# Expert pairs: where one block difference is issued on VectorE, ahead of an addition or behind it

## The chip, the cores and the metric

The kernel runs on one core of one Trainium2 chip. The metric is the device time of one execution in microseconds (us); a time is the median of several executions. The engines are TensorE (PE in the rows; PEld is its weight load), VectorE (DVE), ScalarE (ACT), GpSimd (POOL) and the queue of DMA issues (SP).

## The reference, cut to what matters

Three stages follow each other: an attention over pooled keys, a mixture of eight experts whose gate is balanced by eight rounds of row and column scaling, and a feed-forward layer with softplus. The change lies in the second, whose core is

```python
    out = np.zeros((N, D), dtype=np.float32)
    for e in range(E):
        h = np.maximum(x @ w1[e], 0.0)
        ye = h @ w2[e]
        out += P[:, e:e + 1] * ye
```

with N = 2304 tokens, D = 512, E = 8 experts and 1024 hidden features each.

## The kernel before

The tokens are cut into three groups of 768. Each group passes the experts once, and the hidden features are taken in units of 256, so that one group has 32 units. Every matrix product is made of three matmuls, of a rounded part ("hi") and a remainder ("lo") of either operand. The first product of a unit, x @ w1, is done by a seven-product scheme for 2 x 2 blocks (Strassen and Winograd): with four blocks of the weights and four of the tokens, seven block products named A11, A22, S2, S1, A12, S3 and S4 take the place of eight. Each is six matmuls of 384 columns, and the additions of their results are done on VectorE.

For the second and third group the kernel goes by pairs of units (`first_twice`, `second_twice`): the second product, h @ w2, is done by the same scheme over the two units of a pair. The pair's four blocks of h and three sums of them are then the seven operands ("forms") of seven form products of twelve matmuls each. There are 16 pairs in a group, 32 in all, and they lie between 640 and 1556 us of the span, apart from the very first units.

The order of issue is written out by hand. For a pair d the sequence is: first product of its even unit, form products 2 to 6 of the pair before, first product of its odd unit, form products 0 and 1 of pair d, first product of the even unit of pair d + 1, and so on. Each engine takes its instructions in this order and waits in front of one whose data are not there.

`first_twice` has two double-bank tiles d1 and d2 of PSUM from a pool of two buffers per kind; pairs take the kinds "R" and "L" in turn, and a form product takes its tile py from a pool of the same two kinds. The products are issued as A11, A22, S2, S1, A12, S3; S4 is issued later, behind the next form product (`go_on`). S2 and then S3 accumulate in the same bank pb. The addition u (`vadd(u1, pb, a)`, line 868) must read S2's result there before S3 is added to it. In the code it stands behind the product S1. In the rows it is `u<-p,za` at line 845.

When the odd unit's blocks are finished, `odd_posts` makes the forms. It puts four steps into a list `later`, which the first product of the next even unit works off:

- s2 copies s3 (a difference of two blocks, made shortly before) to its hi part on ScalarE and takes the remainder on GpSimd;
- s4 subtracts s3 from d1 on VectorE, in PSUM (`p<-p,s`, line 846), and copies the result to the hi part of form 6 on ScalarE;
- s1 adds d2 to a21 on VectorE (`a<-p,a`, line 845), takes the hi part on ScalarE and the remainder on GpSimd. It is the last reader of d2;
- the fourth takes the remainder of form 6 on VectorE (`hlo<-p,hhi`, line 896). It is the last reader of d1.

In the odd units `later` is empty. The last pair's four steps are worked off by a unit of the third stage, in `first`, which issues s4 behind its own addition u.

Of the kernel before, what the change touches and what calls it, by code (L numbers as in the profile page):

```python
# [19 lines left out]
def attention_moe_softplus_kernel(  # L20
# [800 lines left out]
    def product_of(n):  # L821

        whi, wlo = w1_t.pop(n)

        def product(ps, a, b, onto=False):
            hi, lo = xs[b]
            for c in range(2):
                three(
                    ps, (whi[:, a, c, :], wlo[:, a, c, :]), (hi[:, c, :], lo[:, c, :]),
                    c == 0 and not onto, c == 1, onto,  # L830
                )

        return product

    two_t = {}
    later = []

    def run_later():
        while later:
            later.pop(0)()  # L840

    def two_banks(kind, name):
        return banks[kind].tile([P, 2, 512], F32, tag=f"two{kind}", name=name)[:, :, :TB]
# [4 lines left out]
    def first_twice(n, between):  # L848

        product = product_of(n)  # L850
        a, u1 = (zpool.tile([P, TB], F32, tag="z", name=x) for x in ("za", "u1"))
        kind = "RL"[sets[n][3] // 2 % 2]
        d1 = two_banks(kind, "p")
        pa, pd_ = d1[:, 0], d1[:, 1]
        product(pa, A11, "b11")
        between(0)
        product(pd_, A22, "t4")
        nc.scalar.copy(a, pa)
        between(1)
        for _ in range(2):  # L860
            if later:
                later.pop(0)()
        d2 = two_banks(kind, "p")
        pc, pb = d2[:, 0], d2[:, 1]
        product(pb, S2, "t2")
        between(2)
        product(pc, S1, "t1")
        vadd(u1, pb, a)
        run_later()
        between(3)  # L870
        product(pa, A12, "b21", True)
        between(4)
        product(pb, S3, "t3", True)
        vadd(a, pb, a)
        vadd(pb, pc, a)
        vadd(pd_, pd_, a)
        between(5)
        two_t[n] = d1, d2

        def s4():  # L880
            product(pc, S4, "b22", True)
            vadd(pc, pc, u1)

        return s4
# [678 lines left out]
    for step, (what, n) in enumerate(todo):  # L1563
# [3 lines left out]
        if what == "first":  # L1567
# [10 lines left out]
            if twice(n):  # L1578
# [10 lines left out]
                def between(k):  # L1589

                    for _ in range((0, 1, 0, 1, 1, 3)[k]):
                        if to_split:
                            to_split.pop(0)()
                    if u % 2 == 0:
                        if k == 2:
                            settled()
                        if joins and k == 1:
                            joins.pop(0)()
                        return
                    if joins and k == 2:  # L1600
                        joins.pop(0)()
                    if k == 0:
                        sharing[0] = not side
                        pause[0] = 0
                    if not sharing[0]:
                        hook()
                    elif (k == 0 and (u < NU1 - 1 or twice(n + 1))) or not between_chunks[0]:
                        convert()

                away[0] = "LR"[u // 2 % 2]  # L1610
                rest = first_twice(n, between)
                prep_w1(n + 1)
                load_w(1, n + 2)
# [124 lines left out]
```

## Time and profile before

| | us |
|---|---|
| median of 3 runs | 1955.16 |
| lowest and highest run | 1954.87, 1958.92 |
| the profiled execution | 1954.04 |
| its span | 1952.3 |
| TensorE busy in the span | 1928.6 (99%) |
| VectorE busy | 1471.4 (75%) |
| GpSimd busy | 1475.1 (76%) |
| ScalarE busy | 973.6 (50%) |

The busy shares are averages over stages with different limits. Matmuls overlap, and their ends are modelled: each is recorded with about 0.33 us, while they start 0.173 us apart when nothing holds them. The granted clock is 0.999 over the span.

### The profile page before, as it was taken

The numbers are of one execution on the slowest core, as the hardware profiler recorded it, in microseconds if no ns is written. First come the engines' busy times: TensorE is split into PE (matmuls) and PEld (weight loads), VectorE is DVE, ScalarE is ACT, GpSimd is POOL, SyncE is SP. The second block draws the span as 40 slices with busy tenths as digits, with TensorE's granted clock in tenths as the row PEclk, the third lists the DMA queues.
The fourth block names the chain that finished last, engine by engine and source line by source line (L and its number), as shares of the span: only waits on it lengthen the run. The fifth ranks groups of instructions, "written<-read, shape, count | busy, mean of one in ns | idle before, by whom it ended". The sixth has DMA issues, their size and how long they took to land.

```text
span 1952.3 us, 30469 instructions
## 1 busy us (share of the span) xinstructions
PE 1928.6 (99%) x10954; PEld 1794.4 (92%) x10954; DVE 1471.4 (75%) x2339; ACT 973.6 (50%) x1773; POOL 1475.1 (76%) x1142
## 2 busy tenths in 40 slices
PE   9899999999999999999999999999999999999999
PEld 7687888989989999999999999999999999999997
DVE  7775576887667888878988889888789776556455
ACT  6545435433334545545445655455554565565542
POOL 6776667787877788778787798887787879675563
PEclk9999999999999999999999999999999999999999
DMA  7343434555547655554555655555545523523311
GB/s 205 116 150 125 145 125 136 178 178 173 183 151 260 208 165 166 168 181 150 163 176 160 219 168 167 161 174 165 181 153 163 192 93 122 191 89 119 133 65 65
DMA packets 213347, 306.56 MB, mean 157 GB/s; under 512 B 33308, under 2 KB 147532, under 8 KB 212940
## 3 DMA queue, kind: packets, MB, share of 16 engines
q1 hardware_dynamic: 203116, 290.85, 46.4%
q10 hardware_dynamic: 10080, 13.77, 1.9%
q8 instruction: 86, 1.41, 0.3%
q14 instruction: 65, 0.53, 0.1%
HBM read 239.30 MB, written 65.27 MB: 156 GB/s over the span
## 4 chain that ended last, share of the span: by engine, by line
PE 90%; DVE 3%; POOL 2%; ACT 2%; DMA 1%; issue 1%; SPq 0%; ACTq 0%; DVEq 0%; POOLq 0%
PE py L797 45%; PE p L797 42%; POOL w1lo L289 1%; PE px L522 1%; PE s L477 1%; DMA vt<-in_v_dram 1%; PE pa L512 1%; DMA pb<-pd 0%; DVE p L1045 0%; POOL w2lo L289 0%; ACT w1hi L320 0%; DMA w2raw<-td 0%; PE pq L464 0%; ACT xhi L693 0%; DVE za L1045 0%
## 5 line engine op out<-in xcount | busy, mean ns | idle before, releaser
L797 PE MATMUL p<-xhi,w1hi 128*128 128x384 f32 x1680 | 572.7, 341 | 5.1 <-DVE p L1045 1.3
L797 PE MATMUL p<-xlo,w1hi 128*128 128x384 f32 x1680 | 563.0, 335 | 0.1
L797 PE MATMUL p<-xhi,w1lo 128*128 128x384 f32 x1680 | 562.9, 335 | 0.0
L289 POOL TENSOR_TENSOR w2lo<-w2raw,w2hi 128x512 fp32r<-128x512 f32 (+1 forms) x235 | 364.0, 1566 | 113.0 <-ACT w2hi L243 100.0
L289 POOL TENSOR_TENSOR w1lo<-w1raw,w1hi 128x512 fp32r<-128x512 f32 x240 | 239.6, 1021 | 227.0 <-ACT w1hi L320 226.9
L797 PEld LDWEIGHTS p<-xhi,w1hi 128*128 128x128 f32 x1680 | 315.6, 188 | 30.1 <-DVE u L845 14.0
L797 PEld LDWEIGHTS p<-xlo,w1hi 128*128 128x128 f32 x1680 | 315.7, 188 | 5.0 <-DVE xlo L1399 0.4
L797 PEld LDWEIGHTS p<-xhi,w1lo 128*128 128x128 f32 x1680 | 315.5, 188 | 0.0
L289 POOL TENSOR_TENSOR w1lo<-sums,w1hi 128x1024 fp32r<-128x1024 f32 x120 | 289.1, 2409 | 1.9 <-ACT w1hi L320 1.9
L797 PE MATMUL py<-w2hi,hhi 128*128 128x512 f32 x672 | 266.4, 396 | 3.3 <-DVE kbd L420 1.3
L797 PE MATMUL py<-w2hi,hlo 128*128 128x512 f32 x672 | 264.0, 393 | 0.0
L797 PE MATMUL py<-w2lo,hhi 128*128 128x512 f32 x672 | 263.6, 392 | 0.0
L797 PE MATMUL py<-hhi,w2hi 128*128 128x384 f32 x716 | 239.4, 334 | 1.1 <-ACT whi L243 1.1
L797 PE MATMUL py<-hlo,w2hi 128*128 128x384 f32 x716 | 239.2, 334 | 0.0
L797 PE MATMUL py<-hhi,w2lo 128*128 128x384 f32 x716 | 239.2, 334 | 0.0
L845 DVE TENSOR_TENSOR g<-py,g 128x768 f32<-128x768 f32 x210 | 199.6, 950 | 50.1 <-PE py L797 50.1
L892 ACT CAST hhi<-p 128x768 fp32r<-128x768 f32 x128 | 102.8, 803 | 211.0 <-DVE p L889 205.7
L797 PEld LDWEIGHTS py<-w2hi,hhi 128*128 128x128 f32 x672 | 126.4, 188 | 32.9 <-issue 3.6
L797 PEld LDWEIGHTS py<-w2hi,hlo 128*128 128x128 f32 x672 | 126.4, 188 | 27.0
L797 PEld LDWEIGHTS py<-w2lo,hhi 128*128 128x128 f32 x672 | 126.5, 188 | 22.5
L797 PEld LDWEIGHTS py<-hhi,w2hi 128*128 128x128 f32 x716 | 134.4, 188 | 1.5 <-ACT whi L243 1.3
L797 PEld LDWEIGHTS py<-hhi,w2lo 128*128 128x128 f32 x716 | 134.4, 188 | 0.0
(163 smaller groups left out, 3540.3 us busy)
## 6 DMA issues: line engine op xcount, KB each, us to landing
w1raw<-in_moe_w_dram SPq DMA_DIRECT2D x96, 512.0 KB
w2raw<-td SPq DMA_DIRECT2D x128, 256.0 KB
sums<-sd SPq DMA_DIRECT2D x62, 512.0 KB
w2raw<-in_moe_w_dram SPq DMA_DIRECT2D x96, 256.0 KB
w2raw<-in_moe_w_dram SPq DMA_DIRECT2D x32, 512.0 KB
sd<-sums SPq DMA_DIRECT2D x32, 512.0 KB
td<-w2raw SPq DMA_DIRECT2D x64, 256.0 KB
xlo<-xlod SPq DMA_DIRECT2D x35, 384.0 KB
```

The costliest lines, as they stand in the source:

```text
L289: nc.gpsimd.tensor_tensor(o, a, b, op=ALU.subtract)
L477: nc.tensor.matmul(ps[:QP, j * 2 * SP:(j + 1) * 2 * SP], qT[:, j * QP:(j + 1) * QP], kb)
L512: nc.tensor.transpose(pa[:SP, j * QP:(j + 1) * QP], ex[:, 2 * j + h, :], ident[:QP, :QP])
L522: nc.tensor.matmul(px[h * D:(h + 1) * D, :W], vp[:, h, :], aT[:, h, :])
L797: nc.tensor.matmul(ps, lhs[a], rhs[b], start=first and i == 0, stop=last and i == 2, skip_group_check=goes_on,)
L845: vadd = lambda o, x, y: nc.vector.tensor_tensor(o, x, y, op=ALU.add)
L892: nc.scalar.copy(h_slot(q)[0], src)
```

## The change

`first_twice` takes one step of `later` instead of two between the products A22 and S2. With s2 gone, s4 stays in the list and is issued with the others by `run_later()` at line 869, behind the addition u.

```diff
         nc.scalar.copy(a, pa)
         between(1)
-        for _ in range(2):
-            if later:
-                later.pop(0)()
+        if later:
+            later.pop(0)()
         d2 = two_banks(kind, "p")
         pc, pb = d2[:, 0], d2[:, 1]
         product(pb, S2, "t2")
```

## Rows read from the trace of the kernel before

**Rows 1.** Busy time by stretch, the stage of the expert pairs.
```profile
core 0: us, PE busy (x) PEld busy (x) DVE busy (x) ACT busy (x) POOL busy (x), PEclk, DMA share, GB/s
640.00:1556.00 916.00, 914.26 (x5200) 899.57 (x5199) 788.30 (x1066) 475.76 (x758) 738.50 (x513) 1.00 0.54 171
```

**Rows 2.** Waits of the weight loads, 640 to 1556 us.
```profile
engine line waited for: us in total, times, longest us
PEld p L797 <- DVE u L845: 14.0, 48, 0.6
```

**Rows 3.** Timeline of VectorE in one even unit.
```profile
start us, us, engine line op out<-in xcount [idle before <-releaser]
880.77 0.95 DVE L846 TENSOR_TENSOR s<-p,s 128x768 f32<-128x768 f32 x1
881.76 0.97 DVE L846 TENSOR_TENSOR p<-p,s 128x768 f32<-128x768 f32 x1
882.63 0.55 DVE L845 TENSOR_TENSOR u<-p,za 128x384 f32<-128x384 f32 x1
883.10 0.95 DVE L845 TENSOR_TENSOR a<-p,a 128x768 f32<-128x768 f32 x1
883.96 0.95 DVE L896 TENSOR_TENSOR hlo<-p,hhi 128x768 fp32r<-128x768 f32 x1
...
887.73 0.57 DVE L845 TENSOR_TENSOR p<-p,u 128x384 f32<-128x384 f32 x1 [0.29 <-PE p L797]
```

**Rows 4.** Timeline of the weight loads in that unit.
```profile
882.71 0.19 PEld L797 LDWEIGHTS p<-xhi,w1lo 128*128 128x128 f32 x1
883.23 0.19 PEld L797 LDWEIGHTS p<-xhi,w1hi 128*128 128x128 f32 x1 [0.33 <-DVE u L845]
...
884.22 0.19 PEld L797 LDWEIGHTS py<-hhi,w2hi 128*128 128x128 f32 x1
```

**Rows 5.** Weight loads: first even unit held, an odd unit, last even unit.
```profile
675.81 0.19 PEld L797 LDWEIGHTS p<-xhi,w1hi 128*128 128x128 f32 x1 [0.33 <-DVE u L845]
...
1534.93 0.19 PEld L797 LDWEIGHTS p<-xhi,w1hi 128*128 128x128 f32 x1 [0.33 <-DVE u L845]
...
930.52 0.19 PEld L797 LDWEIGHTS p<-xhi,w1hi 128*128 128x128 f32 x1 [0.21 <-DVE u L845]
```

**Rows 6.** Timeline of VectorE in the first even unit with `later`.
```profile
643.71 0.97 DVE L846 TENSOR_TENSOR p<-p,s 128x768 f32<-128x768 f32 x1
645.73 0.56 DVE L845 TENSOR_TENSOR u<-p,za 128x384 f32<-128x384 f32 x1 [1.05 <-PE p L797]
646.21 0.95 DVE L845 TENSOR_TENSOR a<-p,a 128x768 f32<-128x768 f32 x1
```

**Rows 7.** Timeline of TensorE there: last matmul of S2, last of S1.
```profile
644.25 0.33 PE L797 MATMUL p<-xhi,w1lo 128*128 128x384 f32 x1
...
645.29 0.33 PE L797 MATMUL p<-xhi,w1lo 128*128 128x384 f32 x1
```

**Rows 8.** Timeline of the weight loads there: first of S3, first of py.
```profile
646.34 0.19 PEld L797 LDWEIGHTS p<-xhi,w1hi 128*128 128x128 f32 x1
...
647.38 0.19 PEld L797 LDWEIGHTS py<-hhi,w2hi 128*128 128x128 f32 x1
```

**Rows 9.** Timeline of VectorE, the last pair's `later` in `first`.
```profile
1563.64 0.55 DVE L1045 TENSOR_TENSOR u<-p,za 128x384 f32<-128x384 f32 x1
1564.11 0.95 DVE L846 TENSOR_TENSOR p<-p,s 128x768 f32<-128x768 f32 x1
1564.97 0.95 DVE L845 TENSOR_TENSOR a<-p,a 128x768 f32<-128x768 f32 x1
1565.93 0.96 DVE L896 TENSOR_TENSOR hlo<-p,hhi 128x768 fp32r<-128x768 f32 x1
```

**Rows 10.** Timeline of all engines, two more even units.
```profile
1120.51 0.56 DVE L845 TENSOR_TENSOR u<-p,za 128x384 f32<-128x384 f32 x1 [1.05 <-PE p L797]
...
1089.77 0.55 DVE L845 TENSOR_TENSOR u<-p,za 128x384 f32<-128x384 f32 x1
...
1090.37 0.19 PEld L797 LDWEIGHTS p<-xhi,w1hi 128*128 128x128 f32 x1
```

**Rows 11.** Timeline of all engines: the closest py load behind `a<-p,a`.
```profile
1416.60 0.95 DVE L845 TENSOR_TENSOR a<-p,a 128x768 f32<-128x768 f32 x1
...
1417.71 0.19 PEld L797 LDWEIGHTS py<-hhi,w2hi 128*128 128x128 f32 x1
```

## The prediction, made before the changed kernel ran

> **What bounds the kernel now.** I read the view by stretch first. The expert pairs run from 640 to 1556 us of the span, and in that stretch TensorE is busy 914.26 of 916.00 us at a granted clock of 1.00, which is the 2.4 GHz level [rows 1]. VectorE is at 788 and GpSimd at 739 of the 916 us, so neither is the bound over the whole stage; time comes or goes only where TensorE waits for one of them inside a unit. A waiting matmul hardly shows as idle time of TensorE, because its weight load waits with it and the matmul before it is still counted as busy. So I read the waits of the weight loads next: 14.0 us in 48 waits, all on the addition u of the expert pairs, and next to nothing else [rows 2].
>
> Then the timeline of one even unit, the only kind in which the changed lines do anything (in an odd unit the list `later` is empty). VectorE has one unbroken queue there: the sum s3 at 880.77, the difference d1 - s3 at 881.76, u at 882.63, the sum a21 at 883.10, the remainder hlo at 883.96 [rows 3]. The product S3 accumulates onto the bank that u reads, so its first weight load waits for u: it starts at 883.23, 0.05 after u ended at 883.18, with 0.33 of idle time in front, 0.52 after the load before it where 0.173 is the usual step [rows 4]. The delay is 0.345. From there to the first load of the next form product the loads need 0.99 [rows 4], against 1.04 in a unit without the wait [rows 8], so 0.05 is regained: **the wait costs 0.29 us.** Of the 31 even units that have something in `later`, 28 show it at 0.32 or 0.33 of idle; the first and the last of them stand in [rows 5]. That is 28 x 0.33 = 9.2 of the 14.0 us; the rest is odd units (0.21 in most of them, as in the third row of [rows 5]) and is not touched by the change. **What the change can win is therefore 28 x 0.29 = 8.1 us.**
>
> **Part by part.** No instruction is added or removed, and no DMA is moved. Of what is popped at line 860, s2 stays: a copy on ScalarE and a remainder on GpSimd, nothing on VectorE. The part s4 moves: one subtraction on VectorE (0.97 as recorded, 0.87 from its start to the next start [rows 3]) and the ScalarE copy of its result. In the new order VectorE gets u, then s4, then a21, then hlo.
>
> *When can u start?* Not as soon as VectorE is free. In the even unit at 640 VectorE had finished d1 - s3 at 644.68 and then stood idle for 1.05 until TensorE released u at 645.73 [rows 6]. The last matmul of S2, whose result u reads, began at 644.25 and lasts 0.33, so it was long done; the last matmul of S1 began at 645.29 and ended at 645.62 [rows 7]. So u waits for the end of S1, behind which it stands in the code, and starts 0.11 later, 0.61 before the first load of S3 (646.34) [rows 6, 8]. There u ends at 646.29 and S3's load starts 0.05 later without a stall. The change leaves u behind S1. In the unit at 883 S3's load without its delay would come at 882.885, so u would start at 882.275, 0.35 earlier than now; VectorE is free for it from about 881.63 (0.86 after s3 began, as between a21 and hlo) and would stand idle for 0.6. This takes the whole 0.29 us away.
>
> *What is queued behind that wait?* VectorE now holds s4 and a21 behind u. The last unit of the stage is followed by a unit of another kind that issues them in just this order: u at 1563.64, s4 at 1564.11, a21 at 1564.97, hlo at 1565.93 [rows 9]. So s4 follows 0.47 after u and a21 another 0.86 after it, and a21 takes 0.95: it ends 2.28 after u starts. Today it starts 0.47 after u. In the unit at 883 it would end at 882.275 + 2.28 = 884.56, against 884.05 now: half a microsecond later, while TensorE has come 0.29 earlier.
>
> *Who waits for a21?* The next form product (k = 2 of the pair before) takes one of the two buffers of that pair's kind, and both hold the odd unit's tiles d1 and d2. hlo still reads d1 until 884.91, while the load of py starts at 884.22 [rows 3, 4]; so py is in the buffer of d2, and the last reader of d2 is a21, which ended at 884.05. Among the 31 units no py load starts less than 0.16 after the end of a21 (the closest: 1417.55 to 1417.71 [rows 11]). Free space today is 0.17 less the 0.05 that a release takes.
>
> *The sum.* Undisturbed, py's first load comes 1.04 after that of S3, that is 0.61 + 1.04 = 1.65 after the start of u [rows 6, 8]. In the new order it may start 2.28 + 0.05 = 2.33 after it. The delay is 0.68, of which 0.05 to 0.06 is regained as above: **0.62 us lost at each py in place of 0.29 at each S3.** For the 28 units: 28 x (0.62 - 0.29) = +9.2 us. The three other even units have little or nothing to win: at 640 and at 1120 u waits for TensorE already today and s4 fills VectorE's idle time ahead of it [rows 6, 10]; put behind u it makes a21 0.87 later there, past a space of 0.2, for 0.62 each. In the third, at 1090, TensorE had itself been late: S3's load came 0.05 after u ended, but without idle time on record [rows 10], so next to nothing (0.04) is to be won there and the same 0.62 to be lost. Together +1.8. The sum is +11.0 to +11.1 us, on the profiled execution's 1954.04 (span 1952.3): 1965.1. The median of the runs, 1955.16, lies 1.1 above that execution, so **1966.2 us**.
>
> *What comes after.* The copy of s4's result on ScalarE starts when s4 ends and takes 0.80, so hlo follows a21 by 0.96 rather than 0.86 [rows 9]; the additions behind it start about 5.7 after u, when S4's product, itself late with py, ends at about 5.8. Today VectorE waits 0.29 for that product [rows 3]. I cost this at nothing; without that cover it could add up to 0.1 in a unit, 3 us in all. The lower bound of the a21 term lets the release of py take no time rather than 0.05: 0.57 lost rather than 0.62, 1.6 us less in all.
>
> One rule speaks for more. VectorE took s4 at 1564.11 while u, begun at 1563.64, was recorded until 1564.19 [rows 9]. The Trainium skill (VectorE: DVE Perf Modes, The DRAIN you can't avoid) says that after every operation the pipeline empties before the next one starts, and adds that an operation that is not held starts earlier. If each waited for the end of the one before, a21 would end 0.55 + 0.97 + 0.95 = 2.47 after u, 0.19 later, and 31 x 0.19 = 5.9 us would come on top: 1972. The rows show the earlier start, in this order of operations.
>
> **The rivals.**
> *A, the forecast:* a21 takes the place of u as the last wait. For it: the two idle waits of u on S1, the order in the last unit, the buffers. 1966.2, own range 1962 to 1971.
> *B, faster:* a21 is not what py needs. Then only u's 8.1 us count: 1955.2 - 8.1 = 1947.1. It decides if py's buffer comes free before a21, or if the buffers are dealt out otherwise. Against it: both buffers are shown occupied, and a space of 0.16 or more in 31 of 31 units; for it: no row shows a py load actually held by a21.
> *C, faster:* u gets going at the end of S2, 1.04 earlier, instead of S1. Then u starts at 881.63, a21 ends at 883.91, py's load is due at 883.93, and nothing is lost: again 1947.1. Against it is u's idle time at 640 and 1120.
> *D, slower still:* py gets the buffer of d1, whose last reader hlo ends about 3.25 after u: 1.6 lost in 31 units, less 8.1, +41: 1997. Against it: the order in which the buffers' last readers are issued, a21 then hlo, is unchanged.
> *E, slower:* each VectorE operation waits for the end of the one before, 1972, as worked out above.
> *F, no change:* the two waits cancel. It would need a loss of 0.26 at py, that is a21 over 0.3 earlier than the rows say.
>
> **How the numbers follow.** Chances: A 0.84, B 0.06, C 0.03, D 0.02, E 0.02, F 0.03. The predicted time is A's. A holds more than the 8 in 10 asked for, and its bounds are 1962 (the 0.57 case, and a run to run scatter of 1 us and more) and 1971 (3 us for VectorE's later additions and the same scatter). About 0.2% or 4 us is what a measurement can tell from no change. Faster: B and C, 0.09. Within 0.2%: F, 0.03. Slower: A, D, E, 0.88.
>
> **What would show it.** Right: weight loads of p no longer wait for u in even units, and 31 loads of py wait about 0.6 for the sum a21; u shows some 0.6 of idle time ahead of it until TensorE; the odd units' 0.21 remain. Pairs come about 0.33 further apart. Wrong: py loads without a wait (B or C, told apart by u's start against S1), py loads that wait for hlo (D), or waits of 0.87 and more (E).

## The result: 11.6 us slower, and where they lie

| | us |
|---|---|
| kernel before, median of five runs (the three above and two more) | 1954.87 |
| changed kernel, median of five runs | 1966.46 |
| changed kernel, lowest and highest | 1965.19, 1970.26 |
| ratio, with its 95% interval | 1.0059 [1.0047, 1.0070] |
| forecast | 1966.2 (1962 to 1971) |
| its profiled execution, span | 1970.26, 1968.5 |

The profiled execution of the changed kernel lies 3.8 above its median. The view by stretch shows that this is not the change's doing. I cut both spans at the start of the first addition u of an expert pair (618.5 before, 623.3 after) and at the start of the last addition of the stage that stands at line 845 (1578.3 and 1594.6). Before:

```profile
core 0: us, PE busy (x) PEld busy (x) DVE busy (x) ACT busy (x) POOL busy (x), PEclk, DMA share, GB/s
0.00:618.50 618.50, 602.63 (x3672) 522.15 (x3673) 433.08 (x847) 283.80 (x615) 458.84 (x409) 1.00 0.50 159
618.50:1578.30 959.80, 956.92 (x5432) 940.14 (x5431) 823.71 (x1117) 499.13 (x794) 774.69 (x542) 1.00 0.55 174
```

After:

```profile
0.00:623.30 623.30, 607.45 (x3672) 527.08 (x3673) 433.07 (x846) 283.56 (x615) 458.68 (x409) 1.00 0.49 157
623.30:1594.60 971.30, 958.05 (x5432) 940.50 (x5431) 826.55 (x1117) 499.13 (x794) 774.51 (x542) 1.00 0.54 172
```

The stage of the expert pairs has grown from 959.8 to 971.3, by 11.5, with the same number of instructions and the same granted clock. The 4.8 ahead of it belong to work that the change doesn't reach, and they are scatter: in the eight experiments below, whose edits don't reach that work either, it ends between 618.2 and 624.0. So the stage carries the whole difference of the medians.

Which wait carries it is shown by the waits of the weight loads in the changed kernel, 640 to 1570 us (before: [rows 2]):

```profile
engine line waited for: us in total, times, longest us
PEld py L797 <- DVE a L845: 21.0, 31, 0.7
PEld p L797 <- DVE u L845: 5.3, 22, 0.5
```

A wait that didn't exist before, py for a21, stands there 31 times, once in each even unit that has something in `later`, at 0.68 on average. The waits for u have gone from 48 to 22. One even unit shows the two changing places, first on VectorE (the same stretch as [rows 3]):

```profile
888.38 0.95 DVE L846 TENSOR_TENSOR s<-p,s 128x768 f32<-128x768 f32 x1
889.89 0.56 DVE L845 TENSOR_TENSOR u<-p,za 128x384 f32<-128x384 f32 x1 [0.57 <-PE p L797]
890.37 0.95 DVE L846 TENSOR_TENSOR p<-p,s 128x768 f32<-128x768 f32 x1
891.23 0.95 DVE L845 TENSOR_TENSOR a<-p,a 128x768 f32<-128x768 f32 x1
892.18 0.96 DVE L895 TENSOR_TENSOR hlo<-p,hhi 128x768 fp32r<-128x768 f32 x1
```

and then the weight loads of the same unit (before: [rows 4]):

```profile
890.50 0.19 PEld L797 LDWEIGHTS p<-xhi,w1hi 128*128 128x128 f32 x1
...
891.36 0.19 PEld L797 LDWEIGHTS p<-xhi,w1lo 128*128 128x128 f32 x1
892.23 0.19 PEld L797 LDWEIGHTS py<-hhi,w2hi 128*128 128x128 f32 x1 [0.68 <-DVE a L845]
```

VectorE has finished s3 at 889.33 and stands idle for 0.57 until TensorE is through with S1. Then u runs, and the load of S3 follows at 890.50, 0.61 after u began, without a wait. But the difference of the blocks and a21 are queued behind u, a21 ends at 892.18, and the load of py comes 0.05 later instead of a step of 0.173 after the load at 891.36.

### The profile page after: what moved, and what is told of

The parts are those of the page before. It is cut to its first block, busy times and chain, and to the rows that moved or that the text cites. A ratio compares the mean times of both kernels' runs of the same rounds, so it can differ in the third digit from the quotient of the medians.

```text
span 1968.5 us, 30469 instructions
## 1 busy us (share of the span) xinstructions
PE 1934.5 (98%) x10954; PEld 1799.7 (91%) x10954; DVE 1474.2 (75%) x2339; ACT 973.2 (49%) x1773; POOL 1474.6 (75%) x1142
## 4 chain that ended last, share of the span: by engine, by line
PE 87%; DVE 8%; POOL 2%; ACT 2%; issue 1%; DMA 1%; ACTq 0%; DVEq 0%; SPq 0%; POOLq 0%
PE py L797 45%; PE p L797 38%; DVE p L846 1%; DVE a L845 1%; PE s L477 1%; DVE u L845 1%; POOL w1lo L289 1%; PE px L522 1%; PE pa L512 1%; PE pk L432 1%; DMA pb<-pd 0%; DVE p L1044 0%; POOL w2lo L289 0%; PE warm L610 0%; PE pq L464 0%
## 5 line engine op out<-in xcount | busy, mean ns | idle before, releaser
L797 PEld LDWEIGHTS py<-hlo,w2hi 128*128 128x128 f32 x716 | 134.4, 188 | 0.0
```

The lines of the kernel that those rows point to most:

```text
L797: nc.tensor.matmul(ps, lhs[a], rhs[b], start=first and i == 0, stop=last and i == 2, skip_group_check=goes_on,)
```

## The experiments

Each is timed against the kernel before on the same chip in the same series: 1955.34 for the first four, 1957.60 for the next three, 1955.30 for the last. The theory (T1): u's wait for S1 holds everything that stands behind u on VectorE, and of that a21 is what TensorE needs next.

**How much of the cost goes by the time between u and a21.** Two runs shorten s4's subtraction, the one instruction that the change puts between them. The first does half of its columns:

```diff
         def s4():
-            vsub(d1, d1, s3_t())
+            vsub(d1[:, :1], d1[:, :1], s3_t()[:, :1])
             form_hi(q + 6, d1)
```

> The changed kernel with the subtraction of s4 done for one half of its columns only (128x384 instead of 128x768, the second half of d1 - s3 is left out), so that VectorE is held for about 0.47 instead of 0.86 between u and a21. T1: a21 ends 0.47 + 0.47 + 0.95 = 1.89 after u, py is due 1.65 after u, so py loads wait about 0.29 in 31 units and lose 0.23 each: +7.3 - 8.1, that is 1954.1, between 1952.5 and 1956. R1 (form 6 and hlo): its copy and its remainder come only 0.4 earlier and stay behind u, so most of the 11.6 us stay, 1961 or more.

Measured: 1954.69, ratio 0.9995 [0.9986, 1.0004]. VectorE's order is kept, and a21 starts 0.94 after u instead of 1.34:

```profile
886.42 0.56 DVE L845 TENSOR_TENSOR u<-p,za 128x384 f32<-128x384 f32 x1 [0.57 <-PE p L797]
886.89 0.56 DVE L846 TENSOR_TENSOR p<-p,s 128x384 f32<-128x384 f32 x1
887.36 0.95 DVE L845 TENSOR_TENSOR a<-p,a 128x768 f32<-128x768 f32 x1
```

```profile
PEld py L797 <- DVE a L845: 8.3, 31, 0.3
PEld p L797 <- DVE u L845: 4.7, 20, 0.6
```

The wait of py fell from 0.68 to 0.27 in each of the 31 units, that is by 0.41, and the time went from 11.6 above the kernel before to 0.65 below it, that is by 12.2, or 0.39 for each unit. The second run leaves the subtraction out:

```diff
         def s4():
-            vsub(d1, d1, s3_t())
             form_hi(q + 6, d1)
```

> The changed kernel without the subtraction of s4 (d1 is used in place of d1 - s3); the copy on ScalarE and the remainder hlo stay where they are. T1: a21 follows u after 0.47 as in the kernel before, with u on time: neither wait is left in the even units, 1946.8, between 1945 and 1949. A rival R3 (only the number of VectorE's instructions behind u counts, not a21): 31 x 0.86 less than the changed kernel, 1940 or less.

Measured: 1948.13, ratio 0.9962 [0.9949, 0.9975]. No py load waits for a21, and no even unit's S3 for u; the waits for u that are left are 20 (5.3 us). So the first 0.41 is worth 12.2 us and the rest of s4 only 6.6, since beyond 0.27 no wait is left to shorten. This is what T1 says; if simply VectorE's load behind u counted (R3), the second half would have brought as much as the first. These two runs leave out a part of the work and are measures of a wait, not kernels to use.

**Whether u's wait for S1 can be taken away.** One line is moved:

```diff
-        product(pc, S1, "t1")
         vadd(u1, pb, a)
+        product(pc, S1, "t1")
         run_later()
```

> The changed kernel with one line moved: the addition u is issued directly behind the product S2, ahead of S1, so that it needn't wait for S1. The order on VectorE (u, s4, a21, hlo) stays that of the changed kernel. Theory T1 (u's wait for S1 holds s4 and a21 back, and a21 holds the load of py): u starts as soon as VectorE is free, about 0.65 earlier, a21 ends at least as early as in the kernel before, no py load waits for a21 by more than 0.1 and no p load of an even unit waits for u; time 1946.8 (1954.9 less 8.1), between 1945 and 1949. Rival R1 (it is the order that costs: with s4 behind u, form 6, its copy on ScalarE and the remainder hlo come late, whatever u waits for): the 11.6 us stay, 1964 to 1967. Rival R2 (u must have S1 finished for a reason other than where it is issued): u starts no earlier, 1966.

Measured: 2068.99, ratio 1.0583 [1.0565, 1.0602]. No theory of mine expected this. On VectorE it went as T1 said: u follows s3 without idle time, and s4 and a21 are early enough; no py load waits for a21.

```profile
916.84 0.95 DVE L846 TENSOR_TENSOR s<-p,s 128x768 f32<-128x768 f32 x1
917.70 0.55 DVE L845 TENSOR_TENSOR u<-p,za 128x384 f32<-128x384 f32 x1
918.17 0.96 DVE L846 TENSOR_TENSOR p<-p,s 128x768 f32<-128x768 f32 x1
919.03 0.95 DVE L845 TENSOR_TENSOR a<-p,a 128x768 f32<-128x768 f32 x1
```

But the weight loads show what TensorE pays for it:

```profile
PEld p L797 <- DVE u L845: 104.8, 63, 2.3
```

```profile
916.70 0.19 PEld L797 LDWEIGHTS p<-xhi,w1lo 128*128 128x128 f32 x1
918.30 0.19 PEld L797 LDWEIGHTS p<-xhi,w1hi 128*128 128x128 f32 x1 [1.42 <-DVE u L845]
```

The load at 916.70 is the last of S2, the one at 918.30 the first of S1, and it comes 0.05 after u ended. S2's result pb and S1's target pc are the two banks of one tile, d2, and the program orders whoever reads one against whoever writes the other: issued behind S1, u waits for S1; issued ahead of it, S1 waits for u. That it is the tile, and not u's place in the code, can be read from the kernel before: the third stage (`first`) also issues S2, then u, then S1, but there each block has a tile of its own. S1's first matmul (1628.09) doesn't wait for u there, and u starts 0.10 after the last matmul of S2 (1627.92) ends:

```profile
1627.92 0.33 PE L797 MATMUL p<-xhi,w1lo 128*128 128x384 f32 x1
1628.09 0.33 PE L797 MATMUL p<-xhi,w1hi 128*128 128x384 f32 x1
1628.35 0.56 DVE L1045 TENSOR_TENSOR u<-p,za 128x384 f32<-128x384 f32 x1 [1.47 <-PE p L797]
```

In 23 of the 24 units of that stage S1 begins 0.25 or more ahead of u; in the other, at 1722, transposes stand between the products.

The waits alone don't make up the loss of 114 us. They grew from 14.0 to 104.8, by 91. In the same stage the granted clock, at 1.00 throughout in the kernel before, fell to 0.50 (the 1.2 GHz level) in 16 short stretches. One of them follows a wait of 1.98 that ended at 739.90, with matmuls 0.32 apart in place of 0.173:

```profile
623.20:1698.70 1075.50, 988.70 (x5438) 966.10 (x5439) 825.35 (x1118) 499.64 (x795) 773.43 (x543) 0.97 0.51 155
741.00:744.00 3.00, 3.00 (x11) 3.00 (x11) 0.17 (x1) 0.00 (x0) 3.00 (x3) 0.50 0.20 64
```

Of the pairs with the same 3.71 us of waits, one with such a stretch takes 34.3 us and one without 32.8, so the 16 stretches cost an estimated 25 us.

So R1 is refuted as to the order on VectorE (the same order, and py waits for nothing), and R2 as well, since u did start earlier. In the expert pairs, giving u a tile of its own for S2's result wasn't tried: the two pools hold all of the buffers, and the later steps read d2 as one operand.

The same line moved in the kernel before was meant as a control:

> Control: the kernel before (s4 ahead of u) with the addition u issued directly behind the product S2. T1: in the even units u is held by VectorE's queue, not by TensorE, so it starts when it started and the 28 waits of 0.33 stay; in the odd units the order on VectorE is unchanged too; no change, 1954.9 within 1.5. Rival R4 (u's place behind S1 costs by itself): a gain, 1947 to 1952.

Measured: 2094.07, ratio 1.0714 [1.0690, 1.0738]. Both expectations missed it for the same reason, S1 waiting for u (here s4 stands ahead of u on VectorE, so u comes later still; the clock fell in 11 stretches of the stage):

```profile
PEld p L797 <- DVE u L845: 131.4, 62, 2.4
```

So it is no control; it repeats the finding.

**Whether a21 is all that matters behind u.** s1 goes ahead of s4:

```diff
-        later.extend([s2, s4, s1, lambda: form_lo(q + 6, d1, nc.vector)])
+        later.extend([s2, s1, s4, lambda: form_lo(q + 6, d1, nc.vector)])
```

> The changed kernel with s1 ahead of s4: order u, a21, s4, hlo on VectorE. T1: no py load waits for a21 (it ends 1.42 after u) and no p load for u, so both known waits of the even units are gone; but hlo needs ScalarE's copy of s4's result, which ends about 3.1 after u, so VectorE stands idle for 1.0 in front of hlo, the addition behind S4 comes 1.4 late, and the py loads behind it wait for the additions g that free their buffers, about 1.25 in a unit: 31 x 1.25 - 8.1 = +31, 1986, between 1975 and 1993. If only a21's place matters (R5: nothing but a21 and u holds TensorE): 1947.

Measured: 1991.09, ratio 1.0178 [1.0160, 1.0195]. The size came out near what was expected and R5 is refuted, but the wait is another one:

```profile
PEld p L797 <- DVE p L845: 46.1, 31, 1.6
PEld p L797 <- DVE u L845: 5.0, 22, 0.4
```

```profile
897.73 0.95 DVE L845 TENSOR_TENSOR a<-p,a 128x768 f32<-128x768 f32 x1
898.59 0.96 DVE L846 TENSOR_TENSOR p<-p,s 128x768 f32<-128x768 f32 x1
900.42 0.96 DVE L895 TENSOR_TENSOR hlo<-p,hhi 128x768 fp32r<-128x768 f32 x1 [0.87 <-ACT hhi L891]
```

a21 is early, and py waits for nothing. But hlo stands idle for 0.87 until ScalarE has copied s4's result, and the unit's additions stand behind hlo. I expected the py loads further on to pay for that. It is S4 that pays, and sooner: its product is added to pc, so its first load has to wait until the addition `vadd(pb, pc, a)` has read pc. It waits 1.49 on average in the 31 units:

```profile
902.49 0.19 PEld L797 LDWEIGHTS p<-xhi,w1hi 128*128 128x128 f32 x1 [1.50 <-DVE p L845]
```

This is a third wait in the row, S3 for u, py for a21, S4 for that addition. In the kernel before no row shows it, because S4's load comes 0.32 to 0.40 after that addition has ended.

**Whether all three can be served.** VectorE is free for 0.6 ahead of u, and half of s4 fits in. So s4, its copy and its remainder are cut in halves, with the first half ahead of u and the second behind a21:

```diff
-        def s4():
-            vsub(d1, d1, s3_t())
-            form_hi(q + 6, d1)
+        def s4(c):
+            vsub(d1[:, c], d1[:, c], s3_t()[:, c])
+            nc.scalar.copy(h_slot(q + 6)[0][:, c], d1[:, c])
...
-        later.extend([s2, s4, s1, lambda: form_lo(q + 6, d1, nc.vector)])
+        later.extend([s2, lambda: s4(0), s1, lambda: s4(1), lambda: lo(0), lambda: lo(1)])
```

In `first_twice` two steps go ahead of u as in the kernel before, and `lo(1)`, the second half of hlo, behind the three additions.

> s4 in two halves of its columns (128x384 each, same result): the first stays ahead of u, the second goes behind a21, with the copy on ScalarE and the remainder hlo in halves too; the second half of hlo behind the unit's three additions. Order on VectorE: s3, s4a, u, a21, s4b, hlo a, the additions, hlo b. T1: u is due 0.64 after VectorE comes free, a half of s4 (0.47 and 0.13 of waiting for s3) fits in, so u starts on time; a21 ends 0.47 + 0.95 = 1.42 after u, before py is due at 1.65; the second remainder ends about 4.5 after u, before d1's buffer is wanted at 4.8, and VectorE comes free for the addition behind S4 at 5.25 against 5.16. Neither wait is left in the even units: 1947 against 1955 for the kernel before, between 1945 and 1950. If instead every step of `later` has to be ahead of u to be hidden (R1), 1955 or more.

Measured: 1972.86, ratio 1.0084 [1.0068, 1.0100]. My working had left out one dependence. The first half of hlo needs the copy of the first half, but it was issued behind the copy of the second and waited for that one; the additions and S4 came late once more:

```profile
890.48 0.56 DVE L846 TENSOR_TENSOR p<-p,s 128x384 f32<-128x384 f32 x1
891.84 0.56 DVE L846 TENSOR_TENSOR hlo<-p,hhi 128x384 fp32r<-128x384 f32 x1 [0.81 <-ACT hhi L954]
```

```profile
PEld p L797 <- DVE p L845: 19.7, 31, 0.7
PEld p L797 <- DVE u L845: 5.7, 22, 0.6
```

Beside it ran the same kernel with u also ahead of the work that odd units take in behind S2 (`between(2)` goes behind `vadd(u1, pb, a)`):

> The kernel with s4 in halves, and u issued ahead of the work that the unit takes in behind S2 (in odd units two conversion steps on VectorE, 1.4 in all, stand ahead of u there). T1 taken to the odd units: their 20 waits of 0.21 to 0.55 go too, about 3.9: 1943, between 1941 and 1947; the conversion steps still fit between u and the addition za. If the steps then delay za and what follows it: 1947 or more.

Measured: 1983.00, ratio 1.0132 [1.0114, 1.0150]. The waits for u are gone in the odd units too, and S4's waits have taken their place there:

```profile
PEld p L797 <- DVE p L845: 35.6, 54, 0.7
```

Of its 54 waits, 31 are the even units' of the run before (0.61 to 0.64 each); the 23 others, of 0.69 to 0.71, are odd units. It is the mistake of the change under study in another place: what had filled the time in which VectorE waits for TensorE was put behind that wait.

The last run mends the split. The first half of hlo is issued ahead of the copy of the second half:

```diff
...
+        def s4b():
+            s4(1)
+            lo(0)
+            hi(1)
...
+        later.extend([s2, s4a, s1, s4b, lambda: lo(1)])
```

> The kernel with s4 in halves again, with the first half of hlo issued ahead of the copy of the second half, so that it doesn't wait for that copy. Order on VectorE: s3, s4a, u, a21, s4b, hlo a, za, the two additions, hlo b. T2 (three waits of TensorE stand in a row in an even unit: S3 for u, py for a21, S4 for the addition that reads S1's result; each must be served before it is due): u on time, a21 1.42 after u (due at 1.65), the addition's end 3.6 after u (due at 3.7): none of the three waits is left. VectorE comes to the addition behind S4 at 5.4 against 5.2, 0.1 lost in the py loads behind it at most: 31 x 0.1 - 8.1 = -5, 1950 against 1955, between 1946.5 and 1952.5. If the third wait remains as in the split before (0.64 each), 1965 or more.

Measured: 1951.22 against 1955.30, ratio 0.9978 [0.9969, 0.9988]. VectorE's queue of one even unit has no idle time in front of any step:

```profile
885.29 0.57 DVE L846 TENSOR_TENSOR p<-p,s 128x384 f32<-128x384 f32 x1
885.82 0.56 DVE L845 TENSOR_TENSOR u<-p,za 128x384 f32<-128x384 f32 x1
886.29 0.94 DVE L845 TENSOR_TENSOR a<-p,a 128x768 f32<-128x768 f32 x1
887.16 0.56 DVE L846 TENSOR_TENSOR p<-p,s 128x384 f32<-128x384 f32 x1
887.75 0.56 DVE L846 TENSOR_TENSOR hlo<-p,hhi 128x384 fp32r<-128x384 f32 x1
888.22 0.55 DVE L845 TENSOR_TENSOR za<-p,za 128x384 f32<-128x384 f32 x1
888.80 1.03 DVE L845 TENSOR_TENSOR p<-p,za 128x384 f32<-128x384 f32 x2
889.74 0.55 DVE L846 TENSOR_TENSOR hlo<-p,hhi 128x384 fp32r<-128x384 f32 x1
```

```profile
PEld p L797 <- DVE u L845: 4.9, 20, 0.6
PEld py L797 <- ACT w2hi L243: 1.6, 3, 1.0
```

The waits for u are those of the odd units; in the even units none is left for u, for a21 or for the additions. This kernel beats both, by 4.1 us on the kernel before, timed beside it, and by some 15 on the changed one. The 8.1 to be won in the even units are not reached in full. Most pairs came about 0.25 closer together, where 0.29 was to be won, and three came further apart, by 0.24, 0.54 and 0.90. Three waits on `w2hi` (1.6 us) weren't there before; why the pairs differ otherwise I didn't follow up.

## Why the prediction was right, point by point

- *What can be won.* Forecast: 28 waits for u in even units vanish, 0.29 each. They vanished, but for two. At 801 and at 1161 u came late for another reason, shown here for the first:

```profile
800.55 0.56 DVE L845 TENSOR_TENSOR u<-p,za 128x384 f32<-128x384 f32 x1 [0.91 <-ACT hhi L891]
```

```profile
801.16 0.19 PEld L797 LDWEIGHTS p<-xhi,w1hi 128*128 128x128 f32 x1 [0.34 <-DVE u L845]
```

  The profile names a copy of ScalarE as the last to release it. Why u should need that copy stays open: at 889.89 it started while the same copy ran on until 890.19. This is a new wait that I hadn't foreseen, worth 2 x 0.3 = 0.6.
- *When u starts.* Forecast: 0.61 ahead of S3's load, after 0.6 of idle time until TensorE. Measured: 889.89 and 890.50, 0.57 of idle time.
- *What is queued behind it.* Forecast: a21 ends 2.28 after u starts, by the last unit of the stage [rows 9]. Measured: 889.89 to 892.18, 2.29. Rival E, where each operation waits for the end of the one before, would have made it 2.47; the rows go on showing 0.48 and 0.86 from start to start.
- *Who waits for a21.* Forecast from the two buffers and from what still reads d1. Shown by 31 waits of py on a21, which the kernel before didn't have, and by the two runs that shortened s4. This was the step with the least behind it, since no row of before showed the wait itself.
- *The size.* Forecast 0.68 of delay per unit and 0.62 lost; measured 0.68 of idle time on average (21.0 in 31). With the 0.6 above, 11.06 becomes 11.7, against 11.5 in the stage and 11.6 between the medians.
- *What comes after.* I costed VectorE's later additions at nothing, with about 0.1 of room. The changed kernel's list of waits shows none on them, so that held. But I had set the room by the addition behind S4 and hadn't seen that S4's own load waits for `vadd(pb, pc, a)`. In the changed kernel that load comes 0.05 to 0.07 after the addition's end in all 31 units, where a release takes 0.05: a VectorE queue only a little longer would have shown as a wait. That the prediction came out right in spite of it is luck in part: two of the later runs failed on exactly this.

## What to carry to other kernels

On an engine that works its queue in order, look at what stands behind a waiting instruction before you move anything behind it. The idle time in front of a wait is the cheapest place there is, and the steps that fill it look like the cause of the delay when they overfill it: here 0.35 too much of a step of 0.87. Before reordering, list every wait of the bounding engine in the next few microseconds with its room, not only the one that is late now; where the room is shorter than the step, cut the step.

## What the runs showed of the hardware and the program that I hadn't expected

A product into one bank of a two-bank tile waits in this program for a VectorE read of the other bank: S1's load came 0.05 after u ended, 1.6 after the load before it, and such waits took 104.8 us. With a tile for each block, in the third stage, the same order of issue shows no such wait; no run gave the two banks of the expert pairs tiles of their own.

In the two kernels with the longest waits of TensorE (104.8 and 131.4 us) the granted clock also fell to 0.50 in 16 and 11 stretches of the stage; in none of the other kernels here did it fall in that stage. In the first of the two a pair with such a stretch took 1.5 us longer than one with the same waits and without it. That the waits bring the clock down, and which of them, is not shown.
